# Attention's score and value products in single runs, and lower halves on VectorE during weight conversion, in a fused attention, MLP and expert kernel

## The chip, the cores and the metric

The kernel runs on one core of a Trainium2 chip. The metric is the device time of one execution in microseconds (us), as the median of several runs. Engines are named as the profile names them: PE is TensorE, DVE is VectorE, ACT is ScalarE, POOL is GpSimd, and SP issues most of the DMAs.

## What is computed

Three layers follow one another. Attention has 4 batches, 8 heads, 576 positions and a head width of 64; half of the heads use a local mask of 32 positions, the other half a mask of every 32nd position. The MLP takes 2304 rows of 512 to 2048 and back with a leaky rectifier. Last, each row is sent to one of 8 experts with room for 288 rows each, by a greedy choice over all gate values, and each expert is another two-layer network.

```
scores = where(mask, scale * q @ k.T, -1e9)
x = softmax(scores) @ v            # 32 heads, rows put back to [2304, 512]
g = maximum(0.01 * (x @ w_in), x @ w_in)
x = g @ w_out                      # 2304 x 512 -> 2048 -> 512
out[rows of e] = maximum(x[rows of e] @ w1[e], 0) @ w2[e]
```

## The kernel before, in words

Attention is cut into 16 units, each of two heads of one batch, and each unit into two groups g of query tiles. A group has three tiles of 96 queries (local mask), or two tiles of 126 or three of 108 (strided mask). `attention()` (lines 240 to 293) is a generator that works through 32 groups as a pipeline: in step s it computes the scores of group s, transposes the probabilities of group s - 2 and multiplies those of group s - 3 with the values. `a_tr` (line 114) transposes q and k of the next unit, `a_qk` (line 147) does the score products of one tile and both heads and yields after each tile, then masks and exponentiates all tiles (`score`, lines 156 to 162: a VectorE operation and a ScalarE one for each tile and head). `a_norm` (line 175) normalizes on GpSimd (line 182), `a_pt` (line 185) transposes, with a few idle products on TensorE in the first five units (line 193), and `a_pv` (line 201) does the value products (line 210), yields after the first tile, and splits the result into a rounded upper half xh (line 234) and the rest xl (line 235). These feed the MLP. f32 products appear as two instructions each in the trace.

The float64 MLP weights are turned to f32 by `convert` (line 313): ScalarE once (line 321), VectorE three times (lines 323 to 325), and a new load is issued from GpSimd's queue (lines 307 and 310). `split` (line 345) makes an upper half of a weight tile on ScalarE or VectorE (lines 350, 352) and the lower half on GpSimd (line 353).

`mlp()` (line 491) is a generator over 64 steps of 16 weight tiles and four row blocks. `g1` (lines 374 to 376) is the first product, 12 instructions of 384 columns in one bank, with a maximum on VectorE (line 383) after it; `g2` (lines 398 to 400) is the second, 9 instructions of 512 columns. Each yields after three instructions, seven yields in a step. `chunk1` (lines 421 to 423) is the first product of the later blocks.

The order is written out by hand as generators, and the framework's scheduler places ready instructions by that priority. First attention runs alone, with one conversion step at every tenth yield, until eight groups are done. Then the MLP runs, and a credit for each of its yields lets attention go on by one yield (`next(A)`) when it has come to 1:

```
credit += 0.9 if DONE[0] < 16 else 0      # first 16 steps
credit += 0.5 if DONE[0] < 32 else 0      # steps 16 to 63
```

PSUM has eight banks: one for the first product (tag p1), three for the second product (p2), two for scores (pS) and two for transposes and value products (pT). Before the second product starts, the first units borrow p2: `tag = "p2" if u < 5 and g else "pS"`.

Of the kernel before, what the change touches and what calls it, by code (L numbers as in the profile page):

```python
# [7 lines left out]
F32 = mybir.dt.float32  # L8
# [18 lines left out]
def body(ctx, tc, q, k, v, w_in, w_out, w_gate, w1, w2, out):  # L27
# [119 lines left out]
    def a_qk(u, g):  # L147
        nq, nk, tl = group(u, g)
        n = len(tl)
        tag = "p2" if u < 5 and g else "pS"  # L150
        p = [ps.tile([128, 4, 128], F32, name=f"pS{h}", tag=tag, bufs=BUFS[tag]) for h in range(2)]
        s = at.tile([126, 2, 3, 128], F32, name="sc", tag="sc", bufs=3)
        mx = at.tile([126, 3, 2, 3], F32, name="mx", tag="mx", bufs=4)
        SC[u, g] = s, mx

        def score(i, m):
            for h in range(2):
                nc.vector.tensor_tensor_reduce(s[:nq, h, i, :nk], p[h][:nq, i, :nk], m[:nq, :nk], -0.125,  # L158
                                               3.0e38, OP.add, OP.min, mx[:nq, 0, h, i:i + 1])
                nc.scalar.activation(s[:nq, h, i, :nk], s[:nq, h, i, :nk], AF.Exp,  # L160
                                     bias=mx[:nq, 0, h, i:i + 1], scale=-1.0,
                                     accum_out=mx[:nq, 1, h, i:i + 1])

        for i, (q0, k0, m, _) in enumerate(tl):
            for h in range(2):
                r = slice(64 * h, 64 * h + 64)
                nc.tensor.matmul(p[h][:nq, i, :nk], QK[u][r, 0, 32 + q0:32 + q0 + nq],
                                 QK[u][r, 1, k0:k0 + nk], start=True, stop=True)
            if u < 2 and i:
                nc.tensor.matmul(p[0][:, 3], ident, QK[u][:, 0, 32:160], start=True, stop=True)  # L170
            yield
        for i, t in enumerate(tl):
            score(i, t[2])

# [10 lines left out]
    def a_pt(u, g, h):  # L185
        nq, nk, tl = group(u, g)
        n = len(tl)
        if h == 0:
            PT[u, g] = at.tile([128, 2, 3, 128], F32, name="pt", tag="pt")
        tag = "p2" if u < 5 and h else "pT"  # L190
        p = ps.tile([128, 4, 128], F32, name="pP", tag=tag, bufs=BUFS[tag])
        for _ in range(3 if u < 5 else 0):
            nc.tensor.matmul(p[:, 3], ident, ident, start=True, stop=True)
        for i in range(n):
            nc.tensor.transpose(p[:nk, i, :nq], SC[u, g][0][:nq, h, i, :nk], ident[:nq, :nq])
        if h or EARLY[0]:
            nc.scalar.activation(PT[u, g][:nk, h, :n, :nq], p[:nk, :n, :nq], AF.Copy)
        else:
            nc.vector.tensor_copy(PT[u, g][:nk, h, :n, :nq], p[:nk, :n, :nq])

    def a_pv(u, g):
        b, c = divmod(u, 4)
        nq, nk, tl = group(u, g)
        n = len(tl)
        t = PT.pop((u, g))
        tag = "p1" if u < 2 else "pT"
        p = ps.tile([128, 3 * 126], F32, name="pX", tag=tag, bufs=BUFS[tag])
        for i, tt in enumerate(tl):
            for h in range(2):
                nc.tensor.matmul(p[64 * h:64 * h + 64, i * nq:i * nq + nq], VT[u][:nk, tt[3], h, :],  # L210
                                 t[:nk, h, i, :nq], start=True, stop=True)
            if i == 0:
                yield
        pieces = []
        if c < 2:
            s0 = b * S + 288 * g
            o = 0
            while o < 288:
                j, a0 = divmod(s0 + o, BLK)
                w = min(288 - o, BLK - a0)  # L220
                pieces.append((p[:, o:o + w], *(x[:, c, a0:a0 + w] for x in xtile(j))))
                o += w
        else:
            r0, nr = 14 * g, n * nq // 18
            i0 = 0
            while i0 < 18:
                j, a0 = divmod(b * S + 32 * i0, BLK)
                i1 = min(18, i0 + (BLK - a0) // 32)
                pieces.append((p[:, :n * nq].rearrange("p (r i) -> p r i", i=18)[:, :, i0:i1],
                               *(x[:, c, a0:a0 + 32 * (i1 - i0)].rearrange("p (i r) -> p r i", r=32)[:, r0:r0 + nr]  # L230
                                 for x in xtile(j))))
                i0 = i1
        for src, dh, dl in pieces:
            (nc.scalar.copy if u else nc.vector.tensor_copy)(dh, src)
            nc.vector.tensor_sub(dl, src, dh.bitcast(F32))  # L235
# [4 lines left out]
    def attention():  # L240
# [9 lines left out]
        for s in range(n + 3):  # L250
            cur, mid, old = (seq[x] if 0 <= x < n else None for x in (s, s - 2, s - 3))
            u, g = cur or (99, 0)
            A = a_qk(u, g) if cur else iter(())
            V = a_pv(*old) if old else iter(())
            if u + 1 < 16 and s >= 1:
                a_tr(u + 1, g)
                yield
            if cur:
                next(A)
                yield  # L260
            if mid:
                a_pt(*mid, 0)
                yield
            if cur:
                next(A, None)
                yield
            if old:
                next(V)
                yield
            if u + 1 < 16 and g == 1:  # L270
                a_tr(u + 1, 2)
                yield
            if cur:
                next(A, None)
                yield
            if mid:
                a_pt(*mid, 1)
                yield
            for _ in A:
                pass  # L280
            if s < 1:
                a_tr(u + 1, g)
                yield
            if cur:
                a_norm(u, g)
            for _ in V:
                pass
            if old:
                DONE[0] += 1
            yield  # L290
            if g == 0 and u + 2 < 16:
                a_load(u + 2)
                v_load(u + 2)
# [51 lines left out]
    def split(pool, src, tag, n):  # L345
# [4 lines left out]
            nc.scalar.activation(hi, src, AF.Copy)  # L350
        else:
            nc.vector.tensor_copy(hi, src)  # L352
        nc.gpsimd.tensor_sub(lo, src, hi.bitcast(F32))  # L353
        return hi, lo


# [1 line left out]
    nc.gpsimd.memset(WB, 0.0)  # L358
    L = consts.tile([128, 18, 8], F32, name="L")
    SI, SO, GG, P2 = {}, {}, {}, {}  # L360

    def prep(n):

# [166 lines left out]
    A, Cv = attention(), conversion()  # L530
    bg = []
    for n, _ in enumerate(A):
        if n % 10 == 0:
            next(Cv, None)
        if DONE[0] >= 8:
            break
    credit = 0.0
    for n, _ in enumerate(mlp()):
# [3 lines left out]
        if st < 16:  # L542
            if n == 0:
                next(Cv, None)
            credit += 0.9 if DONE[0] < 16 else 0
        elif st < 64:
            credit += 0.5 if DONE[0] < 32 else 0
        if n == 20:
            for a in range(4):
                nc.sync.dma_start(WB[32 * a:32 * a + 32, :, 8 * a:8 * a + 8], w_gate.rearrange("(b j) e -> j b e", j=32))  # L550
# [138 lines left out]
            return f  # L689

    soon = Soon()

    def pin(x):

        tc.keep_in_program_order(x[0] if isinstance(x, tuple) else x)

    def search():

# [367 lines left out]
```

## Time and profile before

| | us |
|---|---|
| median of 3 runs | 898.53 (898.48 to 899.33) |
| the profiled execution | 891.85 |
| its span | 890.1 |
| PE busy | 842.4 (95%) |
| PE weight loads busy | 710.9 (80%) |
| DVE busy | 544.8 (61%) |
| ACT busy | 441.5 (50%) |
| POOL busy | 492.1 (55%) |

The busy times are over the whole span; the stages differ, so the rows below are taken by stretch. A row of a timeline has the start in the span, the duration, the engine, the line, the operation and how many instructions were merged into it; products overlap in their durations, so costs are read from starts. In tables of waits the first engine is the one that waits.

### The profile page before, as it was taken

What the parts mean: (1) busy time and instruction counts of PE and PEld (TensorE: products, weight loads), DVE (VectorE), ACT (ScalarE), POOL (GpSimd) and SP (SyncE); (2) the same over time, 40 slices, a digit from 0 to 9 for tenths busy, and PEclk for the clock granted to TensorE, in tenths of its full rate; (3) what the DMA queues carried; (4) which work ended last, traced back from release to release, by engine and by line L of the source; (5) the groups of instructions that cost most, each with busy time, mean ns of one, the idle gap of its engine ahead of it and who ended that gap; (6) DMA issues with size and microseconds to landing.
All of it is one profiled execution on the core that took longest, in us unless ns stands there. A gap on an engine that the chain in (4) does not pass through costs nothing. (4 is left out here: it accounts for less than half of the span.)

```text
span 890.1 us, 17029 instructions
## 1 busy us (share of the span) xinstructions
PE 842.4 (95%) x6272; PEld 710.9 (80%) x6272; DVE 544.8 (61%) x1552; ACT 441.5 (50%) x1098; POOL 492.1 (55%) x402
## 2 busy tenths in 40 slices
PE   8799999899999999999999999997999999999994
PEld 5677766677777787788989777775899999899994
DVE  5787888865546565475645546454758878772320
ACT  5787667464546455444555323332544444444641
POOL 2655646564555565544645355575648547558731
PEclk8999989999999999999999999999899999999998
DMA  8587554420122000044000004362546445546510
GB/s 193 145 199 175 143 137 137 129 63 14 29 46 79 17 6 10 1 160 160 1 1 1 19 1 166 109 205 92 166 147 192 147 133 182 173 146 206 181 52 27
DMA packets 95411, 93.18 MB, mean 105 GB/s; under 512 B 66144, under 2 KB 74336, under 8 KB 95328
## 3 DMA queue, kind: packets, MB, share of 16 engines
q1 hardware_dynamic: 87648, 65.88, 26.0%
q0 software_dynamic: 7680, 26.22, 9.6%
q8 instruction: 49, 0.80, 0.4%
q14 instruction: 34, 0.28, 0.1%
HBM read 76.35 MB, written 15.73 MB: 103 GB/s over the span
## 5 line engine op out<-in xcount | busy, mean ns | idle before, releaser
L353 POOL TENSOR_TENSOR lo<-WI,hi 128x512 fp32r<-128x512 f32 x96 | 127.5, 1328 | 98.9 <-DVE hi L352 58.2
L353 POOL TENSOR_TENSOR lo<-WO,hi 128x512 fp32r<-128x512 f32 x96 | 125.9, 1312 | 88.3 <-ACT hi L350 88.1
L859 POOL TENSOR_TENSOR wlo<-raw,whi 128x1024 fp32r<-128x1024 f32 x48 | 116.8, 2445 | 26.7 <-ACT whi L858 21.7
L350 ACT ACTIVATE hi<-WO 128x512 fp32r<-128x512 f32 x96 | 60.6, 631 | 101.3 <-PE q L961 49.2
L374 PE MATMUL p<-xh,hi 128*128 128x384 f32 x192 | 75.7, 395 | 5.3 <-DVE g L383 5.3
L916 PE MATMUL g<-hh,whi 128*128 128x288 f32 x256 | 78.8, 308 | 0.4 <-DVE exl L879 0.4
L893 PE MATMUL g<-exh,whi 128*128 128x288 f32 x256 | 78.6, 308 | 0.0
L894 PE MATMUL g<-exl,whi 128*128 128x288 f32 x256 | 76.8, 301 | 0.0
L917 PE MATMUL g<-hl,whi 128*128 128x288 f32 x256 | 76.2, 298 | 0.4 <-DVE hl L901 0.4
L895 PE MATMUL g<-exh,wlo 128*128 128x288 f32 x256 | 76.3, 298 | 0.0
L918 PE MATMUL g<-hh,wlo 128*128 128x288 f32 x256 | 75.7, 296 | 0.0
L160 ACT ACTIVATE sc<-sc,mx 96x128 f32<-96x128 f32 (+2 forms) x176 | 67.6, 388 | 15.0 <-DVE mx L158 15.0
L858 ACT ACTIVATE whi<-raw 128x1024 fp32r<-128x1024 f32 x64 | 67.3, 1053 | 2.9 <-DMA raw<-in_moe_w_dram 2.9
L376 PE MATMUL p<-xh,lo 128*128 128x384 f32 x192 | 66.3, 345 | 1.4 <-POOL lo L353 1.2
L421 PE MATMUL p<-xh,hi 128*128 128x384 f32 x192 | 66.4, 346 | 0.0
L375 PE MATMUL p<-xl,hi 128*128 128x384 f32 x192 | 65.8, 343 | 0.2 <-DVE xl L235 0.2
L423 PE MATMUL p<-xh,lo 128*128 128x384 f32 x192 | 64.7, 337 | 0.7 <-POOL lo L353 0.7
L398 PE MATMUL p<-hi,gh 128*128 128x512 f32 x144 | 64.3, 446 | 0.7 <-ACT gh L384 0.7
L422 PE MATMUL p<-xl,hi 128*128 128x384 f32 x192 | 64.4, 335 | 0.0
L182 POOL TENSOR_TENSOR sc<-sc,mx 96x384 f32<-96x384 f32 (+2 forms) x64 | 52.2, 832 | 21.4 <-DVE mx L180 15.2
L932 POOL DMA_INDIRECT out_dram<-o,idx x24 | 24.3, 1011 | 70.4 <-ACT o L908 58.4
L400 PE MATMUL p<-hi,gl 128*128 128x512 f32 x144 | 57.4, 398 | 0.0
(210 smaller groups left out, 2294.3 us busy)
## 6 DMA issues: line engine op xcount, KB each, us to landing
raw<-in_moe_w_dram SPq DMA_DIRECT2D x64, 512.0 KB
wraw<-in_moe_w_in_dram POOLq DMA_DIRECT2D x16, 512.0 KB
wraw<-in_moe_w_out_dram POOLq DMA_DIRECT2D x16, 512.0 KB
g<-g3d SPq DMA_DIRECT2D x16, 384.0 KB
rawq<-in_q_dram SPq DMA_DIRECT2D x32, 144.0 KB
rawk<-in_k_dram SPq DMA_DIRECT2D x32, 144.0 KB
x2d<-x SPq DMA_DIRECT2D x18, 256.0 KB
g3d<-gh SPq DMA_DIRECT2D x16, 192.0 KB
```

The source lines that it names most:

```text
L160: nc.scalar.activation(s[:nq, h, i, :nk], s[:nq, h, i, :nk], AF.Exp, bias=mx[:nq, 0, h, i:i + 1], scale=-1.0, accum_out=mx[:nq, 1, h, i:i ...
L353: nc.gpsimd.tensor_sub(lo, src, hi.bitcast(F32))
L374: nc.tensor.matmul(p1, wh[:, cs], xh[:, c], start=(c == 0), stop=False)
L421: nc.tensor.matmul(p1, wh[:, cs], xh[:, c], start=(c == 0), stop=False)
L858: pin(nc.scalar.activation(hi, raw, AF.Copy))
L859: pin((nc.vector if n in (5, 7) else nc.gpsimd).tensor_sub(lo, raw, hi.bitcast(F32)))
L893: nc.tensor.matmul(p, wh, xh[:, c], start=(c == 0), stop=False)
L894: nc.tensor.matmul(p, wh, xl[:, c], start=False, stop=False)
L895: nc.tensor.matmul(p, wl, xh[:, c], start=False, stop=(c == 3))
L916: nc.tensor.matmul(p, wh, hh[:, j], start=(j == 0), stop=False)
L917: nc.tensor.matmul(p, wh, hl[:, j], start=False, stop=False)
L918: nc.tensor.matmul(p, wl, hh[:, j], start=False, stop=(j == 7))
```

## The change

`a_qk` yields once, after all tiles of the group, and then goes on to the masking; `a_pv` has no yield and does its whole group at once. `attention()` takes the score products in one step, the masking goes ahead of the value products, and a group counts as done right behind these. A step of the pipeline then has five or six yields where it had eight or nine, and the credits and the spacing of conversion steps are changed with that. Units below 4 in place of 5 borrow p2. `split` subtracts on VectorE until the last conversion step has begun. The function `pin` is moved to an earlier place in the file.

```
     def a_qk(u, g):
-        tag = "p2" if u < 5 and g else "pS"
+        tag = "p2" if u < 4 and g else "pS"
...
-            yield
+        yield
         for i, t in enumerate(tl):
             score(i, t[2])
...
-        tag = "p2" if u < 5 and h else "pT"
+        tag = "p2" if u < 4 and h else "pT"
...
             for h in range(2):
                 nc.tensor.matmul(p[64 * h:64 * h + 64, i * nq:i * nq + nq], VT[u][:nk, tt[3], h, :],
                                  t[:nk, h, i, :nq], start=True, stop=True)
-            if i == 0:
-                yield
...
             A = a_qk(u, g) if cur else iter(())
-            V = a_pv(*old) if old else iter(())
...
             if cur:
                 next(A, None)
-                yield
             if old:
-                next(V)
+                a_pv(*old)
+                DONE[0] += 1
                 yield
             if u + 1 < 16 and g == 1:
                 a_tr(u + 1, 2)
                 yield
-            if cur:
-                next(A, None)
-                yield
             if mid:
                 a_pt(*mid, 1)
                 yield
-            for _ in A:
-                pass
             if s < 1:
                 a_tr(u + 1, g)
                 yield
             if cur:
                 a_norm(u, g)
-            for _ in V:
-                pass
-            if old:
-                DONE[0] += 1
-            yield
...
-        nc.gpsimd.tensor_sub(lo, src, hi.bitcast(F32))
+        (nc.gpsimd if CONV[0] > 31 else nc.vector).tensor_sub(lo, src, hi.bitcast(F32))
...
-        if n % 10 == 0:
+        if n % 6 == 0:
             next(Cv, None)
...
-            credit += 0.9 if DONE[0] < 16 else 0
+            credit += 0.6 if DONE[0] < 16 else 0
         elif st < 64:
-            credit += 0.5 if DONE[0] < 32 else 0
+            credit += 0.33 if DONE[0] < 32 else 0
```

## Rows read from the trace of the kernel before

**Rows 1.** Busy time by stretch: columns as in the first line.

```profile
core 0: us, PE busy (x) PEld busy (x) DVE busy (x) ACT busy (x) POOL busy (x), PEclk, DMA share, GB/s
0.00:48.00 48.00, 39.31 (x313) 30.35 (x313) 32.45 (x133) 31.07 (x112) 23.40 (x36) 0.89 0.72 171
48.00:190.00 142.00, 131.20 (x887) 99.41 (x885) 117.17 (x320) 98.69 (x309) 81.58 (x85) 0.96 0.54 142
190.00:390.00 200.00, 200.00 (x1446) 157.67 (x1445) 111.05 (x348) 101.60 (x295) 106.83 (x96) 1.00 0.14 36
390.00:890.00 500.00, 471.92 (x3632) 423.45 (x3630) 284.12 (x754) 210.09 (x384) 280.30 (x187) 0.98 0.37 115
```

**Rows 2.** The same table for line 167 alone, the score products.

```profile
190.00:390.00 200.00, 14.74 (x128) 8.56 (x128) 1.00 0.14 36
```

**Rows 3.** The same table for line 210 alone, the value products.

```profile
190.00:390.00 200.00, 14.97 (x176) 8.39 (x176) 1.00 0.14 36
```

**Rows 4.** Timeline of PE, runs among the MLP's products, 238 to 291 us.

```profile
238.73 0.40 PE L400 MATMUL p<-hi,gl 128*128 128x512 f32 x1
239.05 0.39 PE L210 MATMUL pX<-pt,vt 128*64 128x96 f32 x4
239.37 0.50 PE L398 MATMUL p<-hi,gh 128*128 128x512 f32 x1
239.71 0.39 PE L399 MATMUL p<-lo,gh 128*128 128x512 f32 x1
...
243.27 0.55 PE L210 MATMUL pX<-pt,vt 128*64 128x96 f32 x8
...
289.48 0.39 PE L399 MATMUL p<-lo,gh 128*128 128x512 f32 x1
289.71 0.40 PE L400 MATMUL p<-hi,gl 128*128 128x512 f32 x1
290.04 0.46 PE L167 MATMUL pS<-qk 64*96 64x128 f32 x4
290.43 0.50 PE L398 MATMUL p<-hi,gh 128*128 128x512 f32 x1
290.77 0.39 PE L399 MATMUL p<-lo,gh 128*128 128x512 f32 x1
```

**Rows 5.** Timeline of PE, score runs near the end of the first stage.

```profile
52.90 0.46 PE L167 MATMUL pS<-qk 64*96 64x128 f32 x4
...
53.77 1.34 PE L167 MATMUL pS<-qk 64*96 64x128 f32 x20
```

**Rows 6.** Waits of PE, 48 to 190 us: total, times, longest.

```profile
PE p L374 <- DVE g L383: 5.3, 4, 2.4
PE p L376 <- POOL lo L353: 1.2, 2, 0.9
```

**Rows 7.** Groups of POOL, 48 to 190 us: count, busy, mean ns, idle before.

```profile
L353 POOL TENSOR_TENSOR lo<-WI,hi 128x512 fp32r<-128x512 f32 x17 | 23.6, 1390 | 6.5 <-ACT hi L350 6.3
L353 POOL TENSOR_TENSOR lo<-WO,hi 128x512 fp32r<-128x512 f32 x15 | 20.9, 1393 | 4.1 <-ACT hi L350 4.0
L182 POOL TENSOR_TENSOR sc<-sc,mx 96x384 f32<-96x384 f32 x14 | 12.3, 896 | 2.4 <-DVE mx L180 1.9 <-ACT cg L321 0.4
```

**Rows 8.** Instructions of lines 323 and 324, whole span: shortest, median, longest.

```profile
L323 DVE TENSOR_SCALAR cg<-cg x32: 411/429/3244, 10.5 to 178.4; 128x512 int32<-128x512 int32 x32
...
L324 DVE SCALAR_TENSOR_TENSOR cg<-wraw,cg x32: 644/693/3458, 11.0 to 178.9; 128x512 int32<-128x512 int32 x32
```

**Rows 9.** Timeline around a long conversion step.

```profile
109.36 3.46 DVE L324 SCALAR_TENSOR_TENSOR cg<-wraw,cg 128x512 int32<-128x512 int32 x1
...
109.76 1.27 POOL L353 TENSOR_TENSOR lo<-WI,hi 128x512 fp32r<-128x512 f32 x1
...
111.00 1.27 POOL L353 TENSOR_TENSOR lo<-WO,hi 128x512 fp32r<-128x512 f32 x1
```

**Rows 10.** Groups of DVE, 48 to 190 us, columns as in rows of POOL.

```profile
L324 DVE SCALAR_TENSOR_TENSOR cg<-wraw,cg 128x512 int32<-128x512 int32 x26 | 27.0, 1040 | 0.4
L323 DVE TENSOR_SCALAR cg<-cg 128x512 int32<-128x512 int32 x26 | 19.9, 765 | 7.4 <-ACT cg L321 7.4
```

**Rows 11.** Groups of ACT, 48 to 190 us, the upper halves.

```profile
L350 ACT ACTIVATE hi<-WI 128x512 fp32r<-128x512 f32 x17 | 10.5, 625 | 2.2 <-DVE WI L325 1.7 <-PE p L375 0.3
```

More of the change, by code (lines that the diff above doesn't have):

```diff
@@ L149, in a_qk @@
         n = len(tl)
-        tag = "p2" if u < 5 and g else "pS"
+        tag = "p2" if u < 4 and g else "pS"
         p = [ps.tile([128, 4, 128], F32, name=f"pS{h}", tag=tag, bufs=BUFS[tag]) for h in range(2)]
@@ L170, in a_qk @@
                 nc.tensor.matmul(p[0][:, 3], ident, QK[u][:, 0, 32:160], start=True, stop=True)
-            yield
+        yield
         for i, t in enumerate(tl):
@@ L189, in a_pt @@
             PT[u, g] = at.tile([128, 2, 3, 128], F32, name="pt", tag="pt")
-        tag = "p2" if u < 5 and h else "pT"
+        tag = "p2" if u < 4 and h else "pT"
         p = ps.tile([128, 4, 128], F32, name="pP", tag=tag, bufs=BUFS[tag])
@@ L211, in a_pv @@
                                  t[:nk, h, i, :nq], start=True, stop=True)
-            if i == 0:
-                yield
         pieces = []
@@ L253, in attention @@
             A = a_qk(u, g) if cur else iter(())
-            V = a_pv(*old) if old else iter(())
             if u + 1 < 16 and s >= 1:
@@ L265, in attention @@
                 next(A, None)
-                yield
             if old:
-                next(V)
+                a_pv(*old)
+                DONE[0] += 1
                 yield
@@ L272, in attention @@
                 yield
-            if cur:
-                next(A, None)
-                yield
             if mid:
@@ L278, in attention @@
                 yield
-            for _ in A:
-                pass
             if s < 1:
@@ L285, in attention @@
                 a_norm(u, g)
[L286 to L290, printed above, removed]
             if g == 0 and u + 2 < 16:
@@ L352, in split @@
             nc.vector.tensor_copy(hi, src)
-        nc.gpsimd.tensor_sub(lo, src, hi.bitcast(F32))
+        (nc.gpsimd if CONV[0] > 31 else nc.vector).tensor_sub(lo, src, hi.bitcast(F32))
         return hi, lo
@@ L360, in body, with pin @@
     SI, SO, GG, P2 = {}, {}, {}, {}
+    def pin(x):
+        tc.keep_in_program_order(x[0] if isinstance(x, tuple) else x)
     def prep(n):
@@ L532, in body @@
     for n, _ in enumerate(A):
-        if n % 10 == 0:
+        if n % 6 == 0:
             next(Cv, None)
@@ L544, in body @@
                 next(Cv, None)
-            credit += 0.9 if DONE[0] < 16 else 0
+            credit += 0.6 if DONE[0] < 16 else 0
         elif st < 64:
-            credit += 0.5 if DONE[0] < 32 else 0
+            credit += 0.33 if DONE[0] < 32 else 0
         if n == 20:
@@ L691, in body @@
     soon = Soon()
-    def pin(x):
-        tc.keep_in_program_order(x[0] if isinstance(x, tuple) else x)
     def search():
```

## The prediction

> **What bounds the kernel now.** I read the table of the stages first. Four stretches behave differently [rows 1]. Up to 48 us (attention alone) and from 48 to 190 us (attention, weight conversion and the first block of the MLP) TensorE is not full: 39.3 of 48 us and 131.2 of 142 us, with the granted clock at 0.89 and 0.96. From 190 to 390 us (the rest of attention beside MLP blocks 1 and 2) it is busy for all 200 us at clock 1.00, while VectorE has 111, ScalarE 102 and GpSimd 107 us of work. There TensorE's instruction stream is the time, and whatever it loses or gains moves the end by as much. After 390 us nothing is touched by the change.
>
> Next I counted the small products in the full stretch: 128 score instructions [rows 2] and 176 value instructions [rows 3]. One f32 product shows as two instructions, so a pair (two heads) is four. The timeline of TensorE then shows what a run of them costs among the MLP's products [rows 4]. Undisturbed, two 512-column products start 0.23 us apart (289.48 to 289.71). With one score pair between, the two steps from 289.71 to 290.77 take 1.06 us in place of 0.46: the pair costs 0.60. Likewise one value pair costs 0.98 - 0.46 = 0.52 (238.73 to 239.71). Most of that is not the pair itself. A run of eight value instructions lasts 0.55 us, against 0.39 for four, so a second pair adds 0.16. For scores, twenty instructions (five pairs) in one run last 1.34 us and four last 0.46 [rows 5], so a further pair adds (1.34 - 0.46)/4 = 0.22. What is left, 0.60 - 0.22 = 0.38 and 0.52 - 0.16 = 0.36, is paid once for each run, at its two borders.
>
> **The change, part by part.**
>
> Scores in one run. A group (half a unit) has now two or three separate pairs, each followed by a yield, and at a credit of 0.5 a yield some six MLP products come between. After the change the group's pairs stand together. The 128 instructions of the full stretch are units 10 to 15: 32 runs now, 12 then, so 20 x 0.38 = 7.6 us of TensorE.
>
> Value products in one run. The 176 instructions are units 8 to 15, 16 groups of two runs each, which become one: 16 x 0.36 = 5.8 us. Together 13.4 us in the stretch that TensorE fills. Bounds: 11 if a few runs stay apart in the scheduler's order, 14.5 if none does and neighbours gain as well.
>
> The same from 48 to 190 us. Units 6 to 9 lose 14 score runs and units 4 to 7 lose 8 value runs: 14 x 0.38 + 8 x 0.36 = 8.2 us of TensorE. But there it also waits: 5.3 us for VectorE's maximum after the first product and 1.2 us for GpSimd's lower half [rows 6]. Where VectorE ends last, shorter products only lengthen the wait. So this lies between 0 and 8.2 us.
>
> Lower halves on VectorE. While conversion runs, 31 splits (16 of w_in, 15 of w_out) give their subtraction to VectorE. GpSimd takes 1.39 us for one [rows 7]. No such subtraction on VectorE is in this stretch; the nearest row is the 128x512 operation with two inputs in SBUF of line 324, median 0.693 us [rows 8]. That adds 31 x 0.69 = 21.4 us to VectorE, which has 142 - 117.2 = 24.8 us idle there. It also gives something back. A conversion step at 109.36 us took 3.46 us, and two GpSimd subtractions of 1.27 us lie inside it [rows 9]: 0.69 and two such waits make 3.23. Over the stretch line 324 averaged 1.040 us and line 323 0.765 us [rows 10], against medians of 0.693 and 0.429 [rows 8]: 26 x (0.347 + 0.336) = 17.8 us of blocked VectorE time. GpSimd spent 17 x 1.39 + 15 x 1.39 = 44.5 us on subtractions and 12.3 us on the largest form of the normalization [rows 7], so most of those 17.8 us, 14 by these shares, go with the subtractions. VectorE's demand is then 117.2 + 21.4 - 14 = 125 us; bounded by 121 (all of it returned) and 139 (none). It still fits, and no operation of over 1 us is left ahead of the maximum for which TensorE waits.
>
> The Trainium skill (SBUF — State Buffer, section "SBUF: two separate sides") says the port pair that VectorE and GpSimd share is an exclusive lock and the loser blocks for a whole instruction, and it counts a VectorE operation with two SBUF inputs among those that lock out a GpSimd operation reading SBUF. Rows 9 agree with the blocking. It speaks against this part too, since the moved subtractions can still meet the normalization that stays on GpSimd: by the rows the sum is that below, and by the page alone, with nothing returned, it would be 4 us less, 885 us.
>
> I take 4 us for the stretch of 48 to 190 us, half of the 8.2: VectorE is no fuller than 88% (125 of 142), and its long blocks, which make TensorE wait, go, but its demand does not fall. GpSimd's queue loses 31 x 1.39 = 43 us; its weight loads and normalizations stood behind these, and come earlier. Nothing waits longer for it.
>
> The edits at nothing. The fifth unit's second half takes the score banks instead of the second product's: its scores can wait for the scoring of the group before, at most some 2 us, hidden as other products are ready then; in return the second product's banks are free sooner. Credits fall in step with the yields: a unit's two groups had 8 + 9 yields and have 5 + 6, and 0.6/5.5 = 0.109 groups a yield stands against 0.9/8.5 = 0.106; later 0.060 against 0.059. Conversion in the first stage has one step more (ten calls against nine), taken from later. Loads keep their places on SP's queue. The first 48 us already run scores in runs of eight to twelve; I put them at 0, between -2 and +3. The moved helper adds no instruction.
>
> **Sum.** 7.6 + 5.8 + 4 + 0 = 17.4 us. The profiled execution took 891.85 us (span 890.1) and would take 874.4. The median of the runs is 898.53, 6.7 us above the profiled one; the terms are saved instructions and are the same in both, so the forecast is 898.5 - 17.4 = **881 us**. Its own range: 13.4 with -1 to +9.
>
> **Rivals.**
>
> 1. VectorE's queue becomes the bound before 190 us, and the kernel ends slower. The subtraction needs ScalarE's upper half just before it, and VectorE works in order: what was GpSimd's wait for ScalarE (10.3 us before these operations [rows 7]) is now VectorE's, with the maximum, the score reductions and the conversion queued behind. If no blocked time is returned, 24.8 - 21.4 = 3.4 us of idle time are left, and a wait w at each of 31 subtractions costs 31w - 3.4. It eats the 13.4 us at w = 0.54. At a full upper-half copy, 0.625 us [rows 11], it is 16 us: 898.5 + 16 - 13.4 = 901 us. For it: VectorE's queue waits 7.4 us for ScalarE before line 323 already [rows 10]. Against it: the subtraction is placed when the scheduler expects its input, and blocked time is seen to hang on GpSimd. A milder form with half the wait gives about 888 to 893 us.
>
> 2. The first block gains in full: TensorE keeps its 8.2 us, and the 6.5 us of waits for VectorE and GpSimd [rows 6] go with the long blocks: 13.4 + 14.7 = 28, so 870 us. For it: these waits are of the kind that rows 9 explain. Against it: VectorE's demand doesn't fall.
>
> 3. The change doesn't do what it says: the order of instructions comes from a scheduler that lets ready work of other kinds in, so the runs stay split where banks or operands come late. Then only a third of the 13.4 stays: 894 us. Against it: in the first 55 us runs of up to twenty stand together [rows 5] where nothing is put between.
>
> **How the numbers follow.** The forecast 0.62, rival 2 0.13, the mild form of rival 1 0.13, rival 3 0.06, rival 1 in full 0.06. The forecast's own range is 876 to 886; reaching to rival 2 at 870 and to the mild form up to 891 leaves out rival 3, rival 1 in full and a little more, some 0.15. About 0.2% (1.8 us) is what a measurement of this kernel can tell from no change. Faster by more than that: the forecast, rival 2, the mild form and most of rival 3, 0.92; within it 0.03; slower 0.05.
>
> **What would show it.** Right: between the same two points of the MLP, score runs of eight or twelve instructions, 12 runs in units 10 to 15, and value runs whole; the stretch of full TensorE shorter by about 13 us; line 324's counterpart at a mean below 0.85 us; 31 subtractions of about 0.7 us on VectorE. Wrong: idle time on VectorE that ends with ScalarE's upper half, more TensorE waits for VectorE's maximum than 5.3 us, or a granted clock below 0.96 before 190 us; and a full stretch that is as long as before although its runs are merged.

## The result, and the profile after

The changed kernel takes **887.28 us** (median of four runs, 885.65 to 888.31); the kernel before, on the same chip, 898.5 us (897.41 to 899.33). The ratio is 0.9878 with a 95% interval of 0.9857 to 0.9898: 1.2% faster. The forecast was 881, the range 870 to 891. The profiled execution took 888.27 us (span 886.5), against 891.85 (span 890.1) before.

The table of the stages of the changed kernel, in the columns of [rows 1]:

```profile
core 0: us, PE busy (x) PEld busy (x) DVE busy (x) ACT busy (x) POOL busy (x), PEclk, DMA share, GB/s
0.00:48.00 48.00, 36.81 (x270) 28.14 (x270) 31.18 (x124) 28.56 (x101) 15.97 (x29) 0.86 0.73 177
48.00:190.00 142.00, 127.62 (x871) 102.80 (x869) 114.48 (x340) 95.25 (x298) 42.45 (x57) 0.92 0.53 137
190.00:390.00 200.00, 199.20 (x1532) 168.30 (x1533) 119.68 (x375) 111.04 (x321) 114.34 (x102) 1.00 0.15 42
390.00:886.00 496.00, 468.39 (x3603) 420.46 (x3601) 282.04 (x747) 208.82 (x379) 278.49 (x185) 0.98 0.36 114
```

Two things strike the eye beside [rows 1]. In the third stretch the same 200 us hold 1532 TensorE instructions in place of 1446. In the second the granted clock has fallen from 0.96 to 0.92, and in the first TensorE has done 270 instructions in place of 313. So something was won late and something lost early.

Stretches with fixed borders mix the two, so the runs below are compared between points of the program: the first product of the MLP's second step (step 1), that of step 17, that of block 3 (line 421, now 412), and the end of the span. TensorE's timeline gives the first two, the rows of line 412 the third.

| us in the span | step 1 | step 17 | block 3 | end | 1 to 17 | 17 to block 3 | block 3 to end |
|---|---|---|---|---|---|---|---|
| before | 72.9 | 189.6 | 374.3 | 890.1 | 116.8 | 184.7 | 515.8 |
| after | 87.1 | 196.2 | 370.3 | 886.5 | 109.1 | 174.1 | 516.2 |
| difference | +14.2 | +6.6 | -4.0 | -3.6 | **-7.7** | **-10.6** | +0.4 |

Three terms, then: 10.6 us won where TensorE is full, 7.7 us won in the first block, and 14.2 us lost before the MLP's second step.

**The full stretch.** The table of stages between exactly these two points, before and after:

```profile
189.60:374.30 184.70, 184.70 (x1322) 145.16 (x1320) 100.11 (x325) 94.34 (x281) 100.35 (x90) 1.00 0.12 30
```

```profile
196.20:370.30 174.10, 174.10 (x1327) 146.13 (x1325) 100.62 (x327) 95.73 (x282) 100.09 (x90) 1.00 0.14 34
```

TensorE is busy for all of it in both, at clock 1.00, with practically as many instructions. The time went out of the borders of the runs. The timeline of TensorE in the changed kernel, a value run and a score run between products, to set beside [rows 4]:

```profile
231.64 0.39 PE L391 MATMUL p<-hi,gl 128*128 128x512 f32 x1
231.96 0.72 PE L210 MATMUL pX<-pt,vt 128*64 128x96 f32 x12
232.61 0.50 PE L389 MATMUL p<-hi,gh 128*128 128x512 f32 x1
232.94 0.39 PE L390 MATMUL p<-lo,gh 128*128 128x512 f32 x1
...
294.45 0.33 PE L367 MATMUL p<-xh,lo 128*128 128x384 f32 x1
294.72 0.90 PE L167 MATMUL pS<-qk 64*96 64x128 f32 x12
295.55 0.45 PE L365 MATMUL p<-xh,hi 128*128 128x384 f32 x1
295.83 0.34 PE L366 MATMUL p<-xl,hi 128*128 128x384 f32 x1
```

The whole group of three value pairs costs 231.64 to 232.94, less two steps of 0.23: 0.84 us. Split in two it cost 0.52 + 0.68 = 1.20 (0.52 for one pair and 0.16 more for the second). That is the 0.36 of the prediction. Three score pairs cost 294.45 to 295.83, less two steps of 0.175: 1.03 us, against 3 x 0.60 = 1.80; two borders of 0.38 are gone.

Counted in the timelines between these points, the 128 score instructions stand in 32 runs before and in 12 after, the 156 value instructions in 28 and in 14: no run stayed apart. At the prediction's prices that is 20 x 0.38 + 14 x 0.36 = 12.6 us, 2 us more than was measured. A good part of the difference lies with the neighbours. Seven short runs of the gate's products (line 487, now 478) fall in the stretch. Before, six of them stood beside a score or value run and shared a border with it; after, all seven stand alone. One of each kind, before and after:

```profile
294.02 0.34 PE L376 MATMUL p<-xh,lo 128*128 128x384 f32 x1
294.29 0.26 PE L487 MATMUL pl<-lg,sel 128*32 128x24 f32 x8
294.48 0.46 PE L167 MATMUL pS<-qk 64*96 64x128 f32 x4
...
295.16 0.34 PE L375 MATMUL p<-xl,hi 128*128 128x384 f32 x1
```

```profile
214.38 0.40 PE L391 MATMUL p<-hi,gl 128*128 128x512 f32 x1
214.71 0.26 PE L478 MATMUL pl<-lg,sel 128*32 128x24 f32 x8
...
215.18 0.34 PE L366 MATMUL p<-xl,hi 128*128 128x384 f32 x1
```

The pair of runs costs 294.02 to 295.16, less two steps of 0.175: 0.79 us, 0.19 more than a score run alone (0.60). By itself the gate's run costs 214.38 to 215.18, less 0.23 and 0.175: 0.40. Six times the difference makes 1.2 us, an estimate from these two places.

**The first block.** VectorE's groups from 48 to 190 us, to set beside [rows 10]:

```profile
L311 DVE SCALAR_TENSOR_TENSOR cg<-wraw,cg 128x512 int32<-128x512 int32 x26 | 20.3, 782 | 0.4
L310 DVE TENSOR_SCALAR cg<-cg 128x512 int32<-128x512 int32 x26 | 13.2, 507 | 9.0 <-ACT cg L308 8.9
L340 DVE TENSOR_TENSOR lo<-WI,hi 128x512 fp32r<-128x512 f32 x14 | 12.9, 923 | 0.6 <-ACT hi L337 0.2
L340 DVE TENSOR_TENSOR lo<-WO,hi 128x512 fp32r<-128x512 f32 x13 | 10.0, 767 | 1.7 <-ACT hi L337 1.6
```

Lines 324 and 323 (now 311 and 310) have come down from means of 1040 and 765 ns to 782 and 507: 26 x (0.258 + 0.258) = 13.4 us returned, where I had taken 14. The 27 subtractions in the stretch cost 22.9 us and wait 2.3 us. TensorE's waits in the same stretch, beside [rows 6]:

```profile
PE p L365 <- DVE g L374: 5.3, 4, 2.9
PE pP L195 <- ACT qk L134: 2.4, 2, 1.3
PE pX L210 <- ACT pt L197: 2.1, 1, 2.1
```

The wait for GpSimd's lower half is gone, that for VectorE's maximum is as long as it was, and the third row is new; the next paragraphs are about it.

**The start.** Timeline of TensorE in the changed kernel, 60 to 69 us (the bracket is the idle time before the instruction and what ended it):

```profile
60.36 0.86 PE L193 MATMUL pP<-ident 128*128 128x128 f32 x6
...
61.37 0.46 PE L167 MATMUL pS<-qk 64*96 64x128 f32 x4
63.97 0.77 PE L210 MATMUL pX<-pt,vt 108*64 108x108 f32 x10 [2.14 <-ACT pt L197]
...
67.20 1.65 PE L193 MATMUL pP<-ident 128*128 128x128 f32 x6
```

and what ScalarE did meanwhile:

```profile
60.74 0.65 ACT L308 ACTIVATE cg<-wraw 128x512 f32<-128x512 f32 x1
62.99 0.67 ACT L308 ACTIVATE cg<-wraw 128x512 f32<-128x512 f32 x1 [1.60 <-DMA wraw<-in_moe_w_out_dram]
63.56 0.36 ACT L197 ACTIVATE pt<-pP 126x252 f32<-126x252 f32 x1
```

ScalarE's conversion step waits 1.60 us for its weights, the copy of the transposed probabilities stands behind it, and TensorE idles 2.14 us for that copy. Six idle products that took 0.86 us before the gap take 1.65 us after it. The granted clock shows it, before and after, in slices of 10 us:

```profile
60.00:70.00 10.00, 9.36 (x87) 7.42 (x87) 7.38 (x29) 9.12 (x35) 5.94 (x8) 1.00 0.92 214
70.00:80.00 10.00, 9.83 (x69) 8.38 (x69) 7.87 (x24) 9.12 (x28) 5.79 (x6) 1.00 0.56 155
80.00:90.00 10.00, 9.51 (x61) 7.25 (x61) 8.31 (x23) 6.00 (x20) 6.50 (x7) 1.00 0.73 176
```

```profile
60.00:70.00 10.00, 7.61 (x56) 5.68 (x52) 5.82 (x24) 6.77 (x26) 3.46 (x5) 0.81 0.44 106
70.00:80.00 10.00, 10.00 (x55) 7.53 (x54) 3.67 (x19) 5.49 (x19) 3.01 (x4) 0.50 0.65 165
80.00:90.00 10.00, 9.78 (x52) 8.59 (x52) 6.41 (x24) 6.22 (x22) 1.09 (x2) 0.67 0.45 113
```

From 70 to 80 us TensorE is busy throughout at 0.50, the lower of its two levels (1.2 GHz), while VectorE and ScalarE have little to do: from 66 to 87 us ScalarE waits 6.5 us in all for TensorE's transposes. Of its busy time in these 30 us the clock took 0.19 x 7.61 + 0.50 x 10.00 + 0.33 x 9.78 = 9.7 us, an estimate that puts the whole missing share of the clock down as time. Without that, step 1 would begin near 77.5. Step 0 bears this out: its first product (line 374, now 365) starts at 52.2 us in place of 48.2. So some 4 us are lost before step 0, and some 10 between steps 0 and 1, where the clock fell.

### The profile page after: what moved, and what is told of

The parts are those of the page before. It is cut to its first block, busy times and chain, and to the rows that moved or that the text cites. A ratio compares the mean times of both kernels' runs of the same rounds, so it can differ in the third digit from the quotient of the medians.

```text
span 886.5 us, 17045 instructions
## 1 busy us (share of the span) xinstructions
PE 832.0 (94%) x6272; PEld 719.7 (81%) x6272; DVE 547.4 (62%) x1584; ACT 443.7 (50%) x1097; POOL 451.3 (51%) x371
## 5 line engine op out<-in xcount | busy, mean ns | idle before, releaser
L340 POOL TENSOR_TENSOR lo<-WI,hi 128x512 fp32r<-128x512 f32 x80 | 105.6, 1321 | 94.7 <-DVE hi L339 58.3
L340 POOL TENSOR_TENSOR lo<-WO,hi 128x512 fp32r<-128x512 f32 x81 | 104.2, 1288 | 79.4 <-ACT hi L337 79.4
L880 PE MATMUL g<-exh,whi 128*128 128x288 f32 x256 | 79.6, 312 | 0.0
L365 PE MATMUL p<-xh,hi 128*128 128x384 f32 x192 | 73.3, 382 | 6.1 <-DVE g L374 5.6
L412 PE MATMUL p<-xh,hi 128*128 128x384 f32 x192 | 66.2, 345 | 0.0
L389 PE MATMUL p<-hi,gh 128*128 128x512 f32 x144 | 61.4, 426 | 1.0 <-ACT gh L375 1.0
```

What stands on the lines that cost most here:

```text
L340: (nc.gpsimd if CONV[0] > 31 else nc.vector).tensor_sub(lo, src, hi.bitcast(F32))
L365: nc.tensor.matmul(p1, wh[:, cs], xh[:, c], start=(c == 0), stop=False)
L412: nc.tensor.matmul(p1, wh[:, cs], xh[:, c], start=(c == 0), stop=False)
L880: nc.tensor.matmul(p, wh, xh[:, c], start=(c == 0), stop=False)
```

## The experiments

The kernel before was timed again beside each set of runs, and its median lay between 895.3 and 898.1 us (898.5 beside the first result). So kernels of different sets are compared by their ratios to it; 0.001 is 0.9 us. "Masking" below is the VectorE and ScalarE work on a group's scores.

**The kernel before, unaltered.** It gives the spread of the starts.

> The kernel before, unchanged, profiled once more. Its profiled execution took 891.85 us, below all of its timed ones (897.4 to 899.3), and its second MLP step began at 72.9 us. Theory 1 (the gain of the runs is paid back in part by a slower start of 6 to 14 us): if the first profile was a lucky start, this one has its second MLP step near 80 us, about 7 us more in all, and the rest of the span unchanged within 1 us. Rival (the 7 us lie elsewhere, after the first stage, or are spread): the step begins at 73 us again and the stages behind it are longer. The ratio of times must be 1.00.

Measured: 895.12 us (891.58 to 898.13, ten runs), ratio 0.9994 [0.9968, 1.002]. In its profile step 1 begins at 75.2 us, 2.3 later than in the first profile, with a clock of 0.83 from 70 to 80 us, where TensorE was busy for 9.13 us (0.17 x 9.13 = 1.6). That is neither the 80 of theory 1 nor the 73 of its rival. Step 0 starts at 48.2 again. The other stretches repeat: 116.8, 184.7 and 514.5 us. So the two gains above are not scatter, and some 2 us of the 14.2 at the start are.

**Lower halves back on GpSimd, the rest of the change kept.**

```
-        (nc.gpsimd if CONV[0] > 31 else nc.vector).tensor_sub(lo, src, hi.bitcast(F32))
+        nc.gpsimd.tensor_sub(lo, src, hi.bitcast(F32))
```

> The changed kernel with the lower halves back on GpSimd. Theory 1 (the lower halves on VectorE are worth something between the second and the seventeenth MLP step, as they take away VectorE's long blocks, and do not set the start): the second step begins within 3 us of 87 us, the stretch from it to the seventeenth step is 3 to 7 us longer than the 104 us of the changed kernel, the time 888 to 893 us. Rival (VectorE's extra 21 us of work slow the start and the first block): the second step begins at 75 to 80 us, and the time falls to 878 to 883 us.

Measured: 887.17 us (886.5 to 893.12), ratio 0.9907 [0.9878, 0.9935], which overlaps with that of the change as a whole (0.9878 and, below, 0.9856). But the parts move against each other. Step 1 begins at 81.3 (5.8 us earlier), steps 1 to 17 take 120.3 (11.2 more), and step 17 to block 3 takes 174.7. Neither theory has its numbers; the 104 us from which theory 1 started are 109.1 by the table above. The profiled execution took 892.03 us, one of the two longest of six, so its stretches are on the long side. VectorE's groups from 48 to 190 us in this kernel:

```profile
L311 DVE SCALAR_TENSOR_TENSOR cg<-wraw,cg 128x512 int32<-128x512 int32 x25 | 23.6, 943 | 0.4
L310 DVE TENSOR_SCALAR cg<-cg 128x512 int32<-128x512 int32 x25 | 22.2, 889 | 8.2 <-ACT cg L308 8.1
```

With the subtractions back on GpSimd, the two conversion operations are long again. Without the lower halves on VectorE the change keeps its gain in the full stretch, and has none between steps 1 and 17 (120.3 against 116.8).

**The fifth unit keeps the second product's banks.**

```
-        tag = "p2" if u < 4 and g else "pS"
+        tag = "p2" if u < 5 and g else "pS"
...
-        tag = "p2" if u < 4 and h else "pT"
+        tag = "p2" if u < 5 and h else "pT"
```

> The changed kernel with the fifth unit borrowing the second product's banks again. Theory 1a (the start is late because the fifth unit's second half waits for the two score banks and its scores come in pieces): the second MLP step begins 4 to 8 us earlier than 87 us, and the time falls by as much, to 879 to 883 us. Rival (the second product needs the banks early, and the start is late for other reasons): the second step begins at 87 us or later, time 887 to 891 us.

Measured: 904.14 us (900.82 to 908.58), ratio 1.01 [1.0063, 1.0138]: slower than before, and some 20 us slower than the change (1.01 against 0.9878). Steps 1 to 17 take 129.8. The value products of this kernel around that stretch, and nothing of line 210 between the two rows:

```profile
91.97 0.38 PE L210 MATMUL pX<-pt,vt 128*64 128x96 f32 x2
...
174.12 0.71 PE L210 MATMUL pX<-pt,vt 128*64 128x96 f32 x10 [0.24 <-ACT pt L197]
```

Between 92.1 and 174.1 us not one value product runs: attention stands still for the first block. By the code, the transposes of the fifth unit's second half ask for a bank that the second product has taken by then and keeps for 16 steps. So the two lines from 5 to 4 are what lets the rest of the change work.

This run shows one thing more. Step 1 begins at 79.0, 8.1 us earlier than in the change, as theory 1a had it, though the time went the other way. And TensorE has the same idle gap, longer even, without any fall of the clock:

```profile
63.74 0.77 PE L210 MATMUL pX<-pt,vt 108*64 108x108 f32 x10 [2.62 <-ACT pt L197]
```

```profile
60.00:70.00 10.00, 7.38 (x71) 5.97 (x71) 8.33 (x25) 8.98 (x35) 4.32 (x6) 1.00 0.64 152
70.00:80.00 10.00, 8.11 (x73) 6.32 (x73) 8.63 (x38) 8.79 (x33) 2.74 (x4) 1.00 0.71 177
```

So the gap by itself does not bring the clock down, and with the clock at 1.00 a start behind that gap is not as late: step 0 begins at 52.1, as in the change, and step 1 26.9 us after it, where the change took 34.9.

**Lower halves on VectorE alone, in the kernel before.**

```
-        nc.gpsimd.tensor_sub(lo, src, hi.bitcast(F32))
+        (nc.gpsimd if CONV[0] > 31 else nc.vector).tensor_sub(lo, src, hi.bitcast(F32))
```

> The kernel before with the lower halves on VectorE and nothing else. Theory 1 (a gain of 0 to 4 us in the first block, nothing at the start): 894 to 899 us. Rival (VectorE's extra work is the bound before 190 us): 900 to 908 us, with TensorE's waits for VectorE's maximum above 5.3 us.

Measured: 891.75 us (889.73 to 894.41), ratio 0.9937 [0.9916, 0.9958]. Steps 1 to 17 take 110.1 us, 6.7 less than before; step 17 to block 3 takes 184.7, to the tenth what it was. Step 1 begins at 82.9, with a clock of 0.69 from 60 to 70 us. So this part alone brings the gain of the first block and a late start too, and neither theory has its numbers. The start looks as in the change: a conversion operation on ScalarE waits 1.42 us for its weights, the copy stands behind it, and TensorE idles 2.98 us at 64.13 us. In this kernel conversion comes at every tenth yield and the masking stands where it stood before.

Two of the three terms are thus settled: the full stretch belongs to the merged runs, steps 1 to 17 to the lower halves. Some 2 us of the latter gain are the clock, which over these steps was 0.96 in the kernel before and 0.98 in the change: 0.04 x 108.6 against 0.02 x 97.1 us of TensorE's busy time. Whether the freed VectorE brought that about is not shown. The start was open, and the next four runs went to it. One theory was that ScalarE's waits for weight loads set it; another, that the masking now stands ahead of the copies of the value products.

**Conversion at every eighth yield, and at every tenth.**

```
-        if n % 6 == 0:
+        if n % 8 == 0:
```

> The changed kernel with a conversion step at every eighth yield of the first stage in place of every sixth (seven steps there in place of ten). Theory S1 (the start is late because conversion steps stand in ScalarE's queue before their weights have landed; TensorE then idles behind ScalarE and goes on at half clock): ScalarE's waits for weight loads before 75 us fall from 4.1 to below 2 us, the second MLP step begins at 76 to 82 us in place of 87.1; three conversion steps come back in the first block at 1.8 us of VectorE each, so the time is 881 to 886 us. Rival S2 (the start is late because masking and exponentials now stand ahead of the value copies in the order): the second step stays at 85 to 88 us and the time is 887 to 892 us.

> The same with every tenth yield (six conversion steps in the first stage). S1: the second MLP step begins at 75 to 80 us, the stretch from it to the seventeenth step grows by up to 7 us over the changed kernel's 109 us; time 881 to 889 us. S2: the second step stays at 85 to 88 us; time 890 to 895 us.

Measured: at eight 879.88 us (878.8 to 886.78), ratio 0.9845 [0.9798, 0.9892]; at ten 879.59 us (878.71 to 888.15), ratio 0.982 [0.9791, 0.9848]. In the profile of the first, step 1 begins at 76.9 and the clock is 1.00 from 60 to 90 us. The profiled execution of the second happens to be its longest (888.15): step 1 at 83.4, with clocks of 0.54 and 0.61 from 60 to 80 us. There the clock fell behind a gap of 2.32 us at 60.57 us that ended with VectorE's reductions, not with a copy on ScalarE. Its five executions had mean clocks of 0.966, 0.977, 0.982, 0.981 and 0.979 and took 888.2, 881.5, 879.6, 878.7 and 879.2 us. The time goes with the clock within one kernel. Step 0 begins at 52.2 and 50.9, hardly earlier than in the change, and steps 1 to 17 take 113.1 and 115.6 us, 4.0 and 6.5 more, as S1 had it for conversion that is put off. S2's times are not met. S1's start is met in the first profile alone, its bound on the waits is not (2.6 us before 75 us), and both kernels are faster than it gave.

**The first four lower halves on GpSimd.**

```
+    SPLITS = []
...
-        (nc.gpsimd if CONV[0] > 31 else nc.vector).tensor_sub(lo, src, hi.bitcast(F32))
+        (nc.gpsimd if CONV[0] > 31 or len(SPLITS) < 4 else nc.vector).tensor_sub(lo, src, hi.bitcast(F32))
+        SPLITS.append(1)
```

> The changed kernel with the first four lower halves, which run at 25 to 37 us, on GpSimd, the others on VectorE. Theory S3 (part of the late start is these four, 2.8 us of VectorE in a stage where it is 90% busy, ahead of the score reductions; alone they cost the kernel before 8 us of its start): the second step begins 3 to 6 us earlier than 87.1 us and the time is 882 to 885 us. Rival (they take the place of GpSimd's blocking, so nothing is won): 87 us and 886 to 890 us.

Measured: 878.69 us (877.39 to 882.01), ratio 0.9818 [0.9787, 0.9849]. Step 1 begins at 79.6, clock 1.00 from 60 to 90 us, the other stretches as in the change (108.7, 174.1). ScalarE waits 7.2 us for weight loads before 75 us, more than the 4.1 us in the change. So the sum of these waits does not set the start. The direction is S3's, and start and time are both better than it gave.

**Masking after the second transposes.**

```
-            if cur:
-                next(A, None)
             if old:
                 a_pv(*old)
...
             if mid:
                 a_pt(*mid, 1)
                 yield
+            for _ in A:
+                pass
```

> The changed kernel with the masking and exponentials of a group behind the value products and the second transposes, where they stood before; the runs stay whole. S2 (this order is what makes the start late): the second step begins at 78 to 82 us in place of 87.1, time 880 to 884 us. S1: the second step stays within 3 us of 87 us, or later, time 886 to 891 us. The stretch from the seventeenth step to the third block keeps its 174 us in either case.

Measured: **872.43 us** (871.65 to 874.1), ratio 0.9742 [0.9716, 0.9768], the fastest kernel of the study. Step 0 begins at 47.2, 5 us earlier than in the change, step 1 at 76.0 with the clock at 1.00 from 60 to 90 us, steps 1 to 17 take 106.3, and the full stretch 174.0. VectorE's maximum, for which TensorE waited 5.3 us from 48 to 190 us, now costs it 2.7, while a single wait of 2.7 us for ScalarE's upper half is new. Start and time are better than S2 gave. Against the change (0.9878 and, below, 0.9856) the place of the masking was worth 10 to 12 us, about as much as each of the parts that the prediction priced.

**The change once more.**

> The changed kernel once more, unaltered. Theory C1 (the late start belongs to its order of work): the second MLP step starts again at 85 to 89 us in the span, the granted clock is again below 0.85 between 60 and 90 us, and the median is 886 to 889 us. Rival C2 (the start falls out differently from execution to execution, with the clock that TensorE is granted): the second step may start anywhere from 75 to 89 us, earlier where the clock stays at 1.00, and the time follows one to one: at 77 us, as in the kernel with conversion at every eighth yield, it would be some 878 us. Under both, the stretch from step 17 to the first product of block 3 is 173 to 176 us.

Measured: 886.24 us (883.17 to 888.53), ratio 0.9856 [0.9821, 0.9891]. Step 1 begins at 83.8, and the gap is there again (2.29 us at 63.31). Its clock:

```profile
60.00:70.00 10.00, 7.46 (x51) 5.57 (x52) 5.98 (x25) 6.02 (x22) 4.12 (x6) 0.76 0.41 96
70.00:80.00 10.00, 9.97 (x55) 7.27 (x51) 3.89 (x20) 5.85 (x20) 2.35 (x3) 0.56 0.64 148
80.00:90.00 10.00, 9.52 (x65) 8.04 (x65) 9.20 (x27) 7.74 (x27) 2.97 (x4) 1.00 0.48 136
```

The clock took 0.24 x 7.46 + 0.44 x 9.97 = 6.2 us, and 83.8 - 6.2 = 77.6, the same as the 77.5 of the first profile. So the late start belongs to the change (C1), and how late it is goes with the length of the lower clock. Step 1 lies 1.2 us outside what C1 gave for it, and the clock is back at 1.00 after 80 us, which C1 did not expect.

**Both repairs together.** Masking after the second transposes and conversion at every eighth yield.

> Masking after the second transpose, as in the run at 872.4 us, and conversion at every eighth yield as well, as in the run at 879.9 us. Theory S2 (both edits repair the same thing, a first stage in which the copies of the value products stand behind other work): the gains do not add, 869 to 874 us, with the second MLP step at 75 to 78 us. Rival S3 (conversion in the first stage is a cost of its own): a further 4 to 7 us, 865 to 868 us, with the second step at 70 to 72 us.

Measured: 876.24 us (874.56 to 876.88), ratio 0.9745 [0.972, 0.9769]. By the ratio that is the kernel with the masking moved alone (0.9742). Step 1 begins at 75.5, practically the same; steps 1 to 17 take 110.6, 4.3 more. The two repair the same start, if not at the same place: with the sparser conversion alone step 0 still began at 52.2 us, with the masking moved at 47.2, and here at 46.6. S3 falls: with the start repaired the sparser conversion brings nothing. The 876.24 are 2 us above what S2 gave, in a set whose kernel before was 3 us longer than in the set that S2 was worked out from.

**Masking late, all lower halves on GpSimd.**

> Masking after the second transpose, and all lower halves back on GpSimd. Theory L1 (lower halves on VectorE are worth 7 to 11 us between steps 1 and 17, whatever the order of masking): 872.4 + 7 to 11 = 879 to 884 us, with 113 to 118 us between the two steps in place of 106. Rival L2 (they only made room for the masking that stood ahead of the value copies): within 3 us of 872.4.

Measured: 894.2 us (892.96 to 895.59), ratio 0.9951 [0.9929, 0.9973]. Steps 1 to 17 take 117.8 us, 11.5 more than with VectorE: L1, just beyond the upper end of its 7 to 11. The time is 10 us beyond it: step 1 begins at 82.3, 6.3 later, with a clock of 0.59 from 60 to 70 us, and block 3 to the end takes 3.1 us more (516.6; the profiles of this study scatter from 513.2 to 517.8 there). L2 falls. With the masking early, the lower halves are worth 3 to 5 us in the total (0.9907 against 0.9878 and 0.9856), which the intervals do not tell from nothing; with the masking late they are worth 19 us (0.9951 against 0.9742). The parts do not add.

**Idle products ahead of the gap's end.**

```
+        for _ in range(9 if (u, g) == (2, 1) else 0):
+            nc.tensor.matmul(p[:, :128], ident, ident, start=True, stop=True)
         for i, tt in enumerate(tl):
```

> The changed kernel with nine idle products more, ahead of the value products of one group, the one for which TensorE waits 2.1 to 2.3 us at 62 to 64 us. Nothing that the other engines do is changed; TensorE gets about 2.1 us more to do in a place where it has nothing to do. Theory K1 (the half clock after this gap is what makes the start late): the granted clock stays at 1.00 from 60 to 90 us, the second MLP step starts at 76 to 79 us in place of 84 to 87, and the time is 877 to 881 us. Rival K2 (the late work is ScalarE's, and the clock only falls where TensorE has little to do): the clock may rise, but the second step stays at 83 to 88 us and the time at 885 to 889 us.

Measured: 883.97 us (880.77 to 884.77), ratio 0.9841 [0.9809, 0.9873]. The edit did not fill the gap. TensorE's timeline:

```profile
61.16 0.46 PE L167 MATMUL pS<-qk 64*96 64x128 f32 x4
64.43 0.94 PE L209 MATMUL pX<-ident 128*128 128x128 f32 x6 [2.80 <-ACT pt L197]
...
65.37 2.57 PE L209 MATMUL pX<-ident 128*128 128x128 f32 x12
67.87 1.33 PE L212 MATMUL pX<-pt,vt 108*64 108x108 f32 x12
```

The idle products waited for ScalarE's copy too (by the code they write a bank that this copy frees), ran after the gap, and put the value products off to 67.87 (63.97 in the change). And yet the start came earlier. The clock:

```profile
60.00:70.00 10.00, 7.20 (x57) 6.23 (x58) 4.55 (x20) 5.64 (x23) 2.71 (x3) 0.83 0.58 134
70.00:80.00 10.00, 9.57 (x87) 7.33 (x83) 6.25 (x25) 8.41 (x29) 3.96 (x5) 1.00 0.52 133
80.00:90.00 10.00, 9.75 (x69) 8.63 (x70) 9.64 (x30) 7.31 (x24) 2.61 (x4) 1.00 0.67 160
```

It is back at 1.00 by 70 us, and the clock took 0.17 x 7.20 = 1.2 us. Step 1 begins at 81.3, though nine useless products stood in its way; 81.3 - 1.2 - 3.4 (from 64.43 to 67.87) = 76.7 or a little more. Neither theory has its number: K1 gave 76 to 79 and K2 83 to 88. That a start with more TensorE work in it came earlier speaks for K1, that the lower clock is a cause of the late start and no mere sign of it; so does the kernel with the fifth unit's banks, with the gap, the full clock and a start at 79.0. That the idle products brought the clock back is not shown: with the lower halves alone it was back soon too (0.69 from 60 to 70 us, 0.97 from 70 to 80) without them. In the time the gain is not certain: the ratio is lower than the change's 0.9878 and 0.9856, but the intervals overlap.

## Why the prediction was right, and which step of it failed

The direction and the range held; the point is 6 us too low on the medians. That the time fell inside the range is in part luck. It lies outside the forecast's own 876 to 886 us, in what the range had added for the mild form of rival 1, whose cause did not come about. And the two gains came to 10.6 + 7.7 = 18.3 us against 17.4 forecast, the second from another part of the change than forecast, while the start took some 7 of them back (18.3 less the 11.2 between the medians). In the first pair of profiles it took back 14.2 and left 3.6. By its steps:

- **"Together 13.4 us in the stretch that TensorE fills."** The mechanism is shown: every kernel with merged runs takes 173 to 176 us from step 17 to block 3, all three without them 184.7. The size was 10.6. Part of the difference is the stretch: between these points lie all 128 score instructions but 156 of the 176 value instructions, so 14 of the 16 groups, 7.6 + 14 x 0.36 = 12.6 us by the prediction's prices. Of the remaining 2 us some 1.2 are borders that the gate's short runs had shared with the runs that went, which the prediction did not look at; what is left is open (six more transposes, line 195, in two more runs, fall in the stretch after). Rival 3 falls with the count of runs: 12 and 14.
- **"I take 4 us for the stretch of 48 to 190 us"**, as half of the shorter runs' 8.2. Steps 1 to 17 gained 7.7, but from the other part: merging gave nothing there, and the lower halves 6.7 alone and 11.2 inside the change. The blocked time was the right lever, and it came back almost to the microsecond (13.4 against 14). What was wrong is to whom I gave the gain. Rival 2, which had both the shorter runs and the waits gone, did not come about either: the wait for VectorE's maximum stayed at 5.3 us.
- **The rule on the shared port.** The Trainium skill (SBUF — State Buffer, section "SBUF: two separate sides") has the loser of the port pair blocked for as long as the other engine's instruction lasts. The rows agree: with 31 subtractions gone from GpSimd, 26 conversion operations of each kind became 0.26 us shorter in the mean, and long again in the run that put the subtractions back. The prediction's 885 us, with nothing returned, did not follow from that rule. Its other worry did come true: the moved subtractions meet the normalization that stays on GpSimd. Their median is the 0.69 us that was taken, their mean 0.85 (22.9 / 27), and the five longest, 1.10 to 2.23 us, each have an operation of line 182 on GpSimd beside them. So operations of over 1 us were left on VectorE after all.
- **Rival 1** needed a wait of 0.54 us at each subtraction for ScalarE's upper half; the rows show 2.3 us of waits in all 27. It did not happen.
- **"The first 48 us ... I put them at 0, between -2 and +3."** This is the step that failed. Step 1 begins 14.2 us later in one profile and 10.9 in the other (11.9 and 8.6 against the second profile of the kernel before): 3 to 4 us of order, lost before step 0 (52.2 and 51.4 against 48.2), the rest the lower clock between steps 0 and 1. It fell after a gap that a waiting conversion operation on ScalarE made, ahead of a copy; the prediction had no such wait. That it comes of "one step more" is not shown: the kernel with the lower halves alone, without that step, has it too. Nor does the gap decide by itself whether the clock falls. The rows of the stages [rows 1] already showed TensorE at 39.3 of 48 us there, a stretch with slack, where TensorE waits for the other engines and an edit to their order can cost time. The prediction named a clock below 0.96 before 190 us as a sign that it was wrong; it was 0.92, and it is by this step that it showed.
- **"The edits at nothing"** also held the change of units from 5 to 4. It costs nothing, but only because the change has it: without it the kernel is some 20 us slower.

What stays open: the profiled execution of the kernel before took 891.85 us and its other runs 897 to 899, so between the two profiles only 3.6 us of the 11 are seen. Its later runs with 901.9 and 897.1 us had mean clocks of 0.970 and 0.978; whether the longer ones start late in the same way no trace shows. Why the clock stays down for some 3 us in one kernel (0.83 over 10 us), for 20 in another and does not fall at all in a third, after much the same gap, is open too. No run merged the score products alone or the value products alone, so the share of each in the 10.6 us rests on the prices of the rows.

## What to carry to other kernels

Short products between long ones are paid by the run and not by the piece alone: count the borders in the stretch where TensorE is full. Merging gives what the timeline says, less the borders that other short runs had shared with those that go. Where several engines wait for one another, the order of work is the price: the place of the masking, a move of two lines, was worth 10 to 12 us, and parts that were each measured alone did not add. Look in ScalarE's queue for an operation that waits for a load ahead of a copy that TensorE needs; moving it behind the copy would be the next thing to try, which no run here did.

## What the runs showed of the hardware that was not expected

- A border between runs can be shared: the gate's short run cost 0.40 us alone and 0.19 beside a score run.
- After an idle gap of 2.1 to 2.3 us at 62 to 64 us, the granted clock of the changed kernel fell to 0.50 and was not back at 1.00 before some 87 us, though TensorE was busy for 10.00 of 10 us from 70 on and for 9.78 from 80 on. The gap cost 2 us; the clock after it 6 to 10, by the estimate above. In the kernel with the fifth unit's banks a gap of 2.62 us at the same place left the clock at 1.00.
- In the run with 3.4 us of useless products right after such a gap the clock was back at 1.00 by 70 us, 9 to 17 us sooner than in the two profiles of the change, and the second step began 2.5 to 5.8 us earlier (81.3 against 83.8 and 87.1). It is one execution, and that the products did it is not shown.
- The time of one program's executions goes with the granted clock: with conversion at every eighth yield, mean clocks of 0.981, 0.981, 0.979 and 0.967 went with 878.8, 879.1, 880.6 and 886.8 us. The eight runs of the changed kernel all lay between 0.966 and 0.974, those of the fastest kernel at 0.980 and 0.981.
